# First dense layer of batches 1 to 3 by another chained seven-product scheme, in a fused windowed attention and dense kernel

## The chip, the cores and the metric

The kernel runs on one core of one Trainium2 chip. The metric is the device time of a run in microseconds; with one core that core is also the slowest. Several runs are taken and the median counts.

## The reference

Four batches of eight heads, 768 positions, 64 features a head. Each position attends to the 128 positions up to itself and to the first four positions (the sinks). The result is laid out as 3072 rows of 512 and goes through two dense layers with a squared relu between them. Inputs and output are float32.

```python
scores = np.matmul(q, k.transpose(0, 1, 3, 2)) / np.sqrt(64)     # B=4, H=8, S=768, D=64
keep = is_sink | in_window                                       # 4 sinks, window of 128
a = softmax(np.where(keep, scores, -1e9))
x = np.matmul(a, v).transpose(0, 2, 1, 3).reshape(3072, 512)
h = x @ w_in                                                     # 512 x 2048
r = np.maximum(h, 0.0)
out = (r * r) @ w_out                                            # 2048 x 512
```

## The kernel before, in words

**Order.** Nothing is scheduled by a planner at build time. The program records every step as a numbered `Op` (a step may issue one instruction or many), and `Plan.run` emits the steps in the sequence of a list written out by hand, `ORDER`. Each entry is a step's number, then at times an engine letter (`d` VectorE, `a` ScalarE, `g` GpSimd) where the step may run on several, and `+0` or `+1` where it takes a PSUM tile and may choose between two pools. So the queue of each engine is the order of the list, and an instruction that waits holds back all that stand behind it on its engine. `DUMMIES` adds matmuls that compute nothing ahead of seven of the first steps.

**Rooms.** A `Slot` takes a room of a pool and gives it back after its last reader. PSUM is two pools, `att` and `den`, of two rooms each; a room has two banks of 512 float32 columns. In SBUF there are small pools: `expm` (8 rooms, for exps and temporaries), `r` (3, for relu results), `qs` (6), `qr` (5), `sg`, `osb`, `u`.

**Waits inside a tile.** By default two instructions that touch the same tile are ordered. `touch` removes that order for two accesses of one tile that use different banks, when one is a matmul and the other is not, or when both are by different engines and both were recorded with `alone=True` and with different `part` names.

**Stages.** For each batch: loads of q, k and v on GpSimd's and SyncE's queues; transposes of q and k (L507 on TensorE for batches 0 and 1; for batches 2 and 3 by transposing transfers on SyncE's queue, L461); scores per pair of sequence tiles and head pair (L613); exps on ScalarE (L634); masks (L218 GpSimd, L643 and L646 VectorE); values (L682); reciprocals and norms (L698, L699) into `xn_sb`; a bridge that transposes `xn_sb` into `xT` (L731 on TensorE, or transposing transfers). `copy` (L192 ScalarE, L194 VectorE) moves tiles out of PSUM and casts loaded ones. A batch has three pairs of sequence tiles, 256 positions each.

**First dense layer.** Batch 0 does it as written: `layer1`, 192 matmuls (L763), relu, square. Batches 1 to 3 do it by a seven-product scheme for a 2 by 2 block product: `layer1_fast` forms sums of input blocks (`xs`), `weight_sums_in` once forms sums of weight blocks (`wi`, six in tiles of their own, L810, and four in the place of `w_in`, L818), and `quad` does seven products for four blocks of the result. `FAST` says which pairs go together; a lone pair is first spread into `xd` by ScalarE. There are 18 quads. In a quad, PSUM holds one room of two banks, and a float32 tile `t` keeps a running difference:

1. product 1 into bank 0, product 2 into bank 1; `t` is the copy of bank 0, then `t` minus bank 1 (L936)
2. product 5 starts bank 0 again; `t` minus bank 0 (L936); products 4 and 3 add to banks 1 and 0
3. one relu over both banks, 1024 wide (L951 ScalarE, L953 VectorE); its square (L917, L919)
4. products 6 and 7 add to the banks; one custom VectorE sum over both banks with `t`, bounded below by zero, 1024 wide (L963); its square

**Second dense layer.** Pairs 0 and 1 of batch 0 as written (`layer2`, L984); the others by a chained seven-product scheme (`layer2_chain`, L1233), the very last pair by another (`layer2_fast`, L1094), with sums of weights (L1025) formed once. Results are copied to `osb` and stored from SyncE's queue (L1276).

Of the kernel before, what the change touches and what calls it, by code (L numbers as in the profile page):

```python
# [15 lines left out]
ALU = mybir.AluOpType  # L16
# [5 lines left out]
944 0 1 2 7 8 9 10 11 12 13 14 15 16 17 18 945+0 3 5 19 20 21 6 79 22 23 24 25 55d 56d 57+0 58 59d 60a 83+0 85 103+1  # L22
105 26 27 28 62d 61d 63+1 64 67d 68d 65a 69+0 70 71d 72d 66a 84+1 73a 74a 75+1 76 78d 91+0 86 77a 93 80 113+1 87+0
92+1 89 94 95+0 97 115 88 90 96 98 114+1 99+0 101 117 100d 104+0 81+1 102d 107 82 4 29 106g 30 31 32 33 34 35 36 37 38
39 40 41 42 43 44 45 46 127 47 48 49 50 116d 118d 108d 156+0 109+1 119+1 121 111 162+0 110 120 122 112 123+1 125 124d
126d 157a 163a 158a 164a 168+1 165+0 51 52 53 54 177+0 169a 170d 208g 166a 167a 178d 171+1 179a 172a 128+1 131+0 174+0
173a 132a 129d 319 323 321 175d 324 176d 322 130a 320 159+1 133a 160a 161a 278+0 279 136+1 144+0 145+0 280 281 148 138
146 289+1 149d 139d 274 147d 275 282 290 283 291 292 284 276 277 134+1 137+0 135 286a 140 141d 285 287d 293 150+0 151
294 142+1 196+0 192+1 295 143 193 200+1 198a 202a 195d 197 199d 201 203d 297d 194d 296 298a 152+1 154 204+0 205
212+0+1 153a 155d 189+0 215 206a 213 190a 214 207d 186+0 216 191d 248+0 187d 249d 251+1 209 253a 188d 252a 180+1 181d  # L30
250d 182d 183+0 326 184a 185d 300 301 230+0+1 233 299 288 219+0+1 231 220 304+0 210+0 306a 211 222 305 237+0+0 240
232d 325 302 221 303 223 241d 238 239d 311 307 217+1 254+0 224+0 308a 255 309 218 242+0 225 243 452g 422 423 424 425
426 427 428 429 430 431 432 433 434 234g 235+1 226+0 228 310a 227a 229a 314 236 244+0 246 316a 247a 327 313 245d 329
256+0+1 257 315 328 332 317 330 347+1 333+1 348 334 259 335a 337 312 336 331 338 349a 263+1+1 266 264 339 351 340 341a
350 352 435 436 437 258g 438 439 267g 265g 361+0 353 362 354 363d 260g 364 343 365 366 445 440 453 444 441 355a 356a
342a 448 446 449 442 447 443 451 450 318 344 345 357 375+0 358 376 261+0 359 377a 346a 367 368 379 378 262 380 268+0
270+0 381 382 360a 369a 271a 269 370d 371 272 273d 372 383a 389 373 463+0+0 385 386 466 464 390 408+0 409 394+1 395
410a 391 393 387 411 396a 397 412 456+1+0 413 392 414 398 400 415 374d 388a 457 384a 399 504 458 506 465 467 505 508+0
416a 401 418 419 510a 511 402a 654 655 684g 656 657 658 659 660 661 662 663 664 665 672 459 420 460 685 512a 417a 421a
403a 404 468+0 509 405 513 454+1 469 406 507 514a 455 515 461+0 472+1+0 407a 517 523 542 462 518 519 521 544 675 673  # L40
470 473 546+0 475 543 548a 479+0+0 516 520d 549 480 482 550a 524 481d 545 476d 525 483d 547 495+1+0 551 553 496 552a
498 556 674 676 666 667 668 474g 669 670 499g 471 522 679 488+0+0 555 554 526 497d 484+1 557 491 489 671 492g 490g
477+0 500+0 485 478 559 501 561 527+0 528 529d 563 562 493+0 565 558d 494 534 530 535 531d 566+0 567 532 533a 568d 569
564 570 572 571 536 683 682 677 678 486 502 680 711+0+0 487 503 573 574d 537 538 539d 540 681 541 560 714 712 704+0+0
580+0 581 576 577 582d 583 594 584 585 575a 705 707 688+0+0 713g 715g 706g 708g 689 691 578 586 587 626+1 627 588a
628a 612+0 686+0 613 687 630 596 692 690 595 629 631 716+0 717 589a 614a 632 633 579a 634a 635a 615 590 616 597 617
693+0 694 591 618 636 619 637 592 598+1 599 620a 600a 638 593a 601 622 640+0 641 602 623 642a 736 643 603 644 604 646
605 645 709+0 647 624 740+0 639a 621a 606a 648a 742a 649a 607a 608 609 738 737 650 651 743 739 710 610 611d 741
695+0+0 744a 625a 696 698 652 653d 755 697 699 756 757 745 747 746a 749 748 720+0+0 723 759+0 750 700+0 701 761a 762
751 721 752a 763a 760 722g 753 724g 727+0+1 774 775 758 728 730 725+0 766 764 778+1 779 765a 729d 767 776 726 777 768  # L50
731g 732+1 733 718 719 702 703 754 734 735 793 794 785 770 769 798+1 812+0 799 813 780a 771a 800a 814a 781 782a 797
796 786 772 795 815 801 802 816 817 818 803 783 819 784d 787 820a 804 805 789 822 823 829 826 827 828 791 806a 807a
821a 808 809 788 830+0 831 790a 832a 824 825d 810 858+1 811a 834 872+0 844+1 860a 846a 874a 833 835 836 837 873 845
859 876 838a 839a 886 887 888 875 877 861 840 841 848 862 864 792 773 842 863 847 889 849 878 879 890+0 865 843a 880a
850 882 883 851 892a 881a 866d 867d 884 893 894d 868 869 852a 853a 854 855 870 856 895 891 897 896a 885a 900 857d 871d
# [1345 lines left out]
```

## Time and profile before

| What | Value |
|---|---|
| median of 3 runs | 210.87 us (210.46 to 211.46) |
| span of the profiled execution | 208.3 us; no other time of that execution is given |
| instructions | 5924 |
| TensorE matmul / weight load busy | 200.5 us (96%) / 174.3 us (84%) |
| VectorE / ScalarE / GpSimd busy | 173.1 us (83%) / 135.9 us (65%) / 96.4 us (46%) |
| granted TensorE clock | 1.00 throughout |
| moved by transfers | 26.10 MB |

The span runs from the first to the last recorded instruction of one execution; the median is of runs timed as a whole and is 2.6 us longer. PE is TensorE's matmul side and PEld its weight loads, which overlap; DVE is VectorE, ACT ScalarE, POOL GpSimd, SP SyncE. In a timeline row the first number is the start, the second the time from the start to the end of the group, then engine, line, operation, what is written and read, shapes and count; a bracket names the idle time before it and what ended it. In a row by windows the columns are the stretch, its length, and the busy time of PE, PEld, DVE, ACT and POOL with their instruction counts, then the granted clock and the share and rate of the transfers.

### The profile page before, as it was taken

The page shows a single profiled execution, that of the slowest core. Times are in us where ns is not written, and L with a number is a line of the kernel's source. Part 1 is how long each engine was busy: PE and PEld are TensorE (multiplying, and loading weights), DVE is VectorE, ACT ScalarE, POOL GpSimd, SP SyncE. Part 2 cuts the span into 40 slices and gives each one's busy share as a digit, 9 for nine tenths or more (in the row PEclk, how much of TensorE's full clock was granted, in tenths as well). Part 3 has the DMA queues.
Part 4 walks back from the last instruction along what each step waited for, and adds up shares of the span by engine and source line. Part 5 has one row for each costly group of instructions (what it writes and reads, how often), then busy time and mean ns, then how long its engine had stood idle before and what let it go on. Part 6 is the DMA issues. An engine that isn't in the chain of part 4 may idle for free.

```text
span 208.3 us, 5924 instructions
## 1 busy us (share of the span) xinstructions
PE 200.5 (96%) x2476; PEld 174.3 (84%) x2476; DVE 173.1 (83%) x318; ACT 135.9 (65%) x189; POOL 96.4 (46%) x138
## 2 busy tenths in 40 slices
PE   7989999999998999999999998999999999999993
PEld 7658997457986889989878987999888999998893
DVE  6759268867599998999999987999989598999933
ACT  2695888433749589999987047988856248693110
POOL 7999274599599976689356209000043000000000
PEclk9999999999999999999999999999999999999999
DMA  6999999999999999999999945300204203200115
GB/s 190 260 184 207 173 196 215 166 146 142 261 68 148 131 172 137 181 162 121 154 116 220 109 96 134 148 3 0 50 14 145 50 5 113 88 3 0 50 54 201
DMA packets 93994, 26.10 MB, mean 125 GB/s; under 512 B 86800, under 2 KB 91408, under 8 KB 93968
## 3 DMA queue, kind: packets, MB, share of 16 engines
q0 software_dynamic: 69248, 12.59, 80.2%
q1 hardware_dynamic: 24536, 13.01, 27.9%
q8 instruction: 19, 0.31, 0.6%
q10 hardware_dynamic: 184, 0.14, 0.2%
q14 instruction: 7, 0.06, 0.1%
HBM read 27.30 MB, written 6.29 MB: 161 GB/s over the span
## 4 chain that ended last, share of the span: by engine, by line
PE 82%; DVE 5%; DMA 4%; SPq 3%; ACT 2%; issue 2%; DVEq 0%; ACTq 0%
PE py L1233 26%; PE pm L894 23%; PE pm L763 10%; PE py L984 7%; PE po L682 6%; PE ps L613 4%; DMA qr<-in_q_dram 3%; PE pt L507 2%; PE py L1094 2%; SPq L351 2%; DVE t L936 1%; PE px L731 1%; DMA xT<-xn_sb 1%; SPq L461 1%; ACT expm L634 1%
## 5 line engine op out<-in xcount | busy, mean ns | idle before, releaser
L634 ACT ACTIVATE expm<-ps 128x1024 bf16<-128x1024 f32 (+1 forms) x48 | 43.7, 953 | 7.7 <-PE ps L613 7.5
L218 POOL TENSOR_SCALAR_AFFINE_SELECT expm<-expm 128x512 bf16<-128x512 bf16 x34 | 22.7, 705 | 44.2 <-ACT expm L634 40.4
L894 PEld LDWEIGHTS <-w_in_sb 128*128 128x128 bf16 x384 | 32.2, 114 | 2.0 <-issue 1.9
L1233 PEld LDWEIGHTS <-gT_sb 128*128 128x128 bf16 x288 | 27.2, 98 | 4.7 <-issue 1.4
L917 ACT ACTIVATE gT_sb<-r 128x1024 bf16<-128x1024 bf16 x28 | 28.8, 1054 | 2.5 <-DVE r L963 2.3
L894 PE MATMUL pm<-xs,wi 128*128 128x256 bf16 (+1 forms) x288 | 29.2, 246 | 0.1
L192 ACT ACTIVATE osb<-py 128x256 f32<-128x256 f32 (+1 forms) x30 | 11.9, 399 | 25.0 <-PE py L1233 19.8
L936 DVE TENSOR_TENSOR t<-t,pm 128x512 f32<-128x512 f32 x36 | 23.8, 683 | 3.7 <-PE pm L894 2.9
L894 PEld LDWEIGHTS <-wi 128*128 128x128 bf16 x288 | 24.6, 114 | 1.0 <-DVE xs L852 0.4
L1233 PEld LDWEIGHTS <-sg 128*128 128x128 bf16 x216 | 20.3, 98 | 2.7 <-issue 0.5
L963 DVE CUSTOM_DVE_ANT_1 r<-pm,t 128x1024 bf16<-128x1024 f32 x18 | 21.8, 1218 | 0.5 <-PE pm L894 0.5
L763 PE MATMUL pm<-xT,w_in_sb 128*128 128x256 bf16 x192 | 22.0, 273 | 0.0
L763 PEld LDWEIGHTS <-w_in_sb 128*128 128x128 bf16 x192 | 20.6, 114 | 0.3 <-issue 0.2
L894 PE MATMUL pm<-xs,w_in_sb 128*128 128x256 bf16 (+1 forms) x192 | 19.9, 246 | 1.0 <-DVE t L936 1.0
L951 ACT ACTIVATE r<-pm 128x1024 bf16<-128x1024 f32 x16 | 16.3, 1022 | 4.9 <-DVE osb L194 2.3
L1233 PE MATMUL py<-w_out_sb,gT_sb 128*128 128x256 bf16 x144 | 18.7, 273 | 0.6 <-ACT expm L634 0.6
L1233 PE MATMUL py<-wt,sg 128*128 128x256 bf16 x144 | 18.7, 273 | 0.0
L1233 PE MATMUL py<-wt,gT_sb 128*128 128x256 bf16 x144 | 18.5, 273 | 0.0
L682 PEld LDWEIGHTS <-expm 128*128 128x128 bf16 x352 | 16.6, 97 | 1.9 <-issue 0.6
L682 PE MATMUL po<-v,expm 128*128 128x65 bf16 x352 | 17.8, 193 | 0.3 <-ACT expm L634 0.3
L699 DVE TENSOR_TENSOR xn_sb<-po,rc 128x512 bf16<-128x512 f32 (+1 forms) x28 | 17.2, 615 | 1.0
L984 PE MATMUL py<-w_out_sb,gT_sb 128*128 128x512 bf16 x64 | 14.8, 379 | 0.0
(104 smaller groups left out, 376.9 us busy)
## 6 DMA issues: line engine op xcount, KB each, us to landing
out_dram<-osb SPq DMA_DIRECT2D x11, 512.0 KB, 3.7
v<-in_v_dram POOLq DMA_DIRECT2D x24, 128.0 KB, 6.2
qn<-in_k_dram POOLq DMA_DIRECT2D x20, 128.0 KB, 6.1
qn<-in_q_dram POOLq DMA_DIRECT2D x20, 128.0 KB, 6.5
w_in_sb<-in_moe_w_in_dram POOLq DMA_DIRECT2D x4, 512.0 KB, 9.4
w_out_sb<-in_moe_w_out_dram POOLq DMA_DIRECT2D x4, 512.0 KB, 10.8
qr<-in_k_dram SPq DMA_DIRECT2D x4, 256.0 KB, 5.1
qr<-in_q_dram SPq DMA_DIRECT2D x4, 256.0 KB, 4.8
```

The source lines that it names most:

```text
L218: nc.gpsimd.affine_select(out=e_tile, in_=e_tile, compare_op=ALU.is_ge, fill=fill, base=i - 1, pattern=[[0, n], [1 if i else -1, 128]], ch ...
L634: nc.scalar.activation(out=x[:, :, o:512], in_=bank_t["s", b, s, m][:, :, o:512], func=AF.Exp, scale=scale)
L682: touch(("po", b, s, m0), e, nc.tensor.matmul(pv[:, i, h2, :], lhsT=lhsT, rhs=rhs, start=(n_ == 0), stop=(n_ == len(mms) - 1)), j)
L699: touch(("po", b, s, m0), e, nc.vector.tensor_tensor(out=xn_sb[:, 2 * s:2 * s + 2, 128 * (m0 + j0):128 * (m0 + j0 + nj)].rearrange("p i (j ...
L763: nc.tensor.matmul(pm[:, i, :], lhsT=w_in_sb[:, fb // 4, kb, fb % 4:512:4], rhs=xT[:, c0 // 256:(c0 + cw) // 256, kb, :], start=(kb == 0), ...
L894: touch(tag, e, nc.tensor.matmul(y[:, bk, i, :], lhsT=weights(name, f0 + i, a), rhs=rhs[:, a, :], start=fresh and i == 0 and a == 0, stop= ...
L917: nc.scalar.activation(out=d, in_=x, func=AF.Square)
L936: touch(tag, e, nc.vector.tensor_tensor(out=T["t"], in0=T["t"], in1=T["y"][:, bk], op=ALU.subtract), bk)
L951: touch(tag, e, nc.scalar.activation(out=r, in_=T["y"], func=AF.Relu), 0, 1)
L963: touch(tag, e, nc.vector._custom_dve(TENSOR_ADD_SAT, out=r.rearrange("p b n c -> p b (n c)"), in0=T["y"].rearrange("p b n c -> p b (n c)" ...
L984: touch((b, u), e, nc.tensor.matmul(pm[:, i, :], lhsT=gT_sb[:, fb, 128 * t:128 * t + 128], rhs=w_out_sb[:, fb, :], start=(fb == 0), stop=( ...
L1233: touch((b, u), e, nc.tensor.matmul(region(name), lhsT=x[:, i, :], rhs=w_[:, i, :], start=first and i == 0, stop=i == HB - 1, skip_group_c ...
```

## The change

The first layer of batches 1 to 3 keeps 18 quads and seven products each, with another set of block sums. All sums are chained differences: four `xs` tiles of two blocks for each call (before: three of two blocks and one of four), and four `wi` sums in two halves each, eight instructions (before: ten). A quad keeps three copies of bank 0 at different stages instead of a running difference:

1. products 1 and 2 into banks 0 and 1; copy `c1` of bank 0; the bounded sum of bank 1 and `c1` is the first half of `r1`
2. product 6 adds to bank 0 (after `c1` is taken), product 7 starts bank 1 again (after the first sum); copy `c2`; product 5 adds to bank 0; copy `c3`; the bounded sum of bank 1 and `c3` is the second half of `r1`; square
3. products 3 and 4 add to the banks; a relu of bank 0 and the bounded sum of bank 1 and `c2` fill `r2`; square

So a quad has three copies, three custom sums and one relu, all 512 wide, in place of one copy and two differences 512 wide and a relu and a custom sum 1024 wide. Copies, sums and the relu are recorded with `alone=True` and a `part` name each, so that two of them on different engines are ordered only where they use the same bank (or read each other's result). Each copy may be on ScalarE or VectorE, by the letter in `ORDER`; the custom sums are VectorE's.

`ORDER` is new as a whole: 980 entries for 946, since a quad has more steps, in another sequence for every stage of all four batches, with other engine letters and pool choices. The numbers of matmuls are the same. One cast of batch 0's q goes to GpSimd. Only the first lines of the list are shown here.

```diff
 ORDER = """
-944 0 1 2 7 8 9 10 11 12 13 14 15 16 17 18 945+0 3 5 19 20 21 6 79 22 23 24 25 55d 56d 57+0 58 59d 60a 83+0 85 103+1
-105 26 27 28 62d 61d 63+1 64 67d 68d 65a 69+0 70 71d 72d 66a 84+1 73a 74a 75+1 76 78d 91+0 86 77a 93 80 113+1 87+0
+0 8 7 9 978 1 10 6 56d 979+1 11 3 55d 61d 12 57+0 58 13 14 15 19 20 63+0 62d 59a 21 79 60 22 64 103+1 5 65a 66a 104+0
+16 105 23 67d 68d 83+0 4 69+1 70 107 73d 71 75+1 72a 24 77 113+1 85 74 115 76 91+0 78 80 92+0 84+1 114+1 25 93 94 26
...
-    945: 29, 58: 8, 63: 10, 64: 4, 83: 3, 91: 3, 97: 3,
+    979: 29, 58: 8, 63: 10, 64: 4, 83: 3, 91: 3, 97: 3,
...
-        spec = ((1, A[0][0], A[1][1], ALU.add, (0, 0), (0, 1)), (6, A[1][0], A[0][0], ALU.subtract, (0, 2), (1, 0)),
-                (7, A[0][1], A[1][1], ALU.subtract, (1, 1), (1, 2)))
+        spec = ((1, A[1][0], A[1][1], ALU.add, (0, 0), (0, 1)), (2, 1, A[0][0], ALU.subtract, (0, 2), (1, 0)),
+                (4, A[0][1], 2, ALU.subtract, (1, 1), (1, 2)))
...
-        for name, x, y, old in ((2, A[1][0], A[1][1], 6), (5, A[0][1], A[0][0], 7)):
-            for a in range(2):
+        for a in range(2):
+            def run(e, x=A[1][0], y=A[0][0], a=a):
+                wi_sb[3, a] = x[:, :, a]
+                nc.vector.tensor_tensor(out=x[:, :, a], in0=y[:, :, a], in1=x[:, :, a], op=ALU.subtract)
+            ops["wi", 3, a] = op(key + 0.03 + 0.004 * a, {"dve": 0.7}, run, after=[ops["wi", 1, a]] + last)
...
-        total((1,), lambda: part(0, 0), lambda: part(1, 1), ALU.add, 0)
-        total((4,), lambda: part(1, 0), lambda: part(0, 0), ALU.subtract, 1)
-        total((3,), lambda: part(0, 1), lambda: part(1, 1), ALU.subtract, 2)
-        total((6, 7), lambda: halves[0], lambda: halves[1], ALU.add, 3)
+        o1 = total(1, lambda: part(0, 1), lambda: part(0, 0), 0, [])
+        o2 = total(2, lambda: part(1, 1), lambda: xs[1], 1, [o1])
+        total(3, lambda: part(1, 1), lambda: part(0, 1), 2, [])
+        total(4, lambda: part(1, 0), lambda: xs[2], 3, [o2])
...
-        bs, ts, r1s, r2s = Slot(("den", "att"), 1), Slot("expm", 3), Slot("r", 1), Slot("r", 1)
+        bs, r1s, r2s = Slot(("den", "att"), 2), Slot("r", 1), Slot("r", 1)
...
+        def kept(name, n, after):
+            slot = cs[name] = Slot("expm", 1)
+
+            def run(e):
+                T[name] = bank(slot, "t", [128, nb, hw], FP32)
+                touch(tag, e, copy(e, T[name], T["y"][:, 0]), 0, alone=True, part=name)
+            P.group = ("t", b, ss[0])
+            return op(key(n), {"act": 0.6, "dve": 0.69}, run, after=after, takes=[slot])
...
+        def bounded(r, slot, half, name, n, after, takes, reads=()):
+            def run(e):
+                d = rooms_of(r, slot)[:, half]
+                touch(tag, e, nc.vector._custom_dve(
+                    TENSOR_ADD_SAT, out=d.rearrange("p n c -> p (n c)"),
+                    in0=T["y"][:, 1].rearrange("p n c -> p (n c)"),
+                    in1=T[name].rearrange("p n c -> p (n c)"), s0=3.4028235e38, s1=0.0), 1, alone=True, part=name)
+            P.group = ("t", b, ss[0])
+            return op(key(n), {"dve": 0.69}, run, after=after, takes=takes, reads=[cs[name]] + list(reads))
...
         m1 = product(1, 0, 0, True, [])
         m2 = product(2, 1, 1, True, [])
-        k1 = op(key(1), {"act": 0.6, "dve": 0.64}, first, after=[m1], takes=[ts])
-        k2 = op(key(2), {"dve": 0.7}, less(1), after=[m2, k1], reads=[ts])
-        m5 = product(5, 0, 2, True, [k1])
-        k3 = op(key(3), {"dve": 0.7}, less(0), after=[m5, k2], reads=[ts])
-        m4 = product(4, 1, 3, False, [k2])
-        m3 = product(3, 0, 4, False, [k3])
-        k4 = op(key(5), {"act": 1.04, "dve": 1.25}, relu, after=[m3, m4], takes=[r1s])
-        square(6, "r1", f0, 1, r1s, [k4])
-        m6 = product(6, 0, 6, False, [k4])
-        m7 = product(7, 1, 7, False, [k4])
-        k5 = op(key(8), {"dve": 1.25}, final, after=[m6, m7, k3], takes=[r2s], reads=[bs, ts])
-        square(9, "r2", f0 + 8, 1, r2s, [k5])
+        k1 = kept("c1", 1, [m1])
+        e1 = bounded("r1", r1s, 0, "c1", 2, [m2, k1], [r1s])
+        m6 = product(6, 0, 2, False, [k1])
+        m7 = product(7, 1, 3, True, [e1])
+        k2 = kept("c2", 3, [m6])
+        m5 = product(5, 0, 4, False, [k2])
+        k3 = kept("c3", 5, [m5])
+        e4 = bounded("r1", r1s, 1, "c3", 6, [m7, k3], [])
+        square(7, "r1", f0, 0, r1s, [e1, e4])
+        m3 = product(3, 0, 6, False, [k3])
+        m4 = product(4, 1, 7, False, [e4])
...
+        k4 = op(key(7), {"act": 0.6, "dve": 0.69}, relu, after=[m3], takes=[r2s], reads=[bs])
+        e3 = bounded("r2", r2s, 1, "c2", 8, [m4, k2], [], [bs])
+        e3.after.append(k4)
+        square(9, "r2", f0, 1, r2s, [k4, e3])
```

More of the change, by code (lines that the diff above doesn't have):

```diff
@@ L27 @@
[L27 to L36, printed above, removed]
@@ L897, in run @@
                             skip_group_check=not (fresh and i == 0)), bk)
[L898 to L901 removed]
+            wi = {5: 1, 6: 2, 7: 3, 3: 4}.get(name)
+            need = [ops["wi", wi, a] for a in range(2)] if wi else [w_in_op[i] for i in range(4)]
+            o = op(key(n), {"pe": 0.45}, run, after=after + need + ([sums[x]] if x else landed) + last[-1:],
+                   takes=[bs] if name == 1 else [], reads=[slots[x]] if x else [whole] if len(ss) == 1 else [])
             last.append(o)
```

137 lines of the change are left out of this document (62 added, 75 removed).

## The prediction

> **What bounds the kernel now.** I read the page first (the busy shares), then the busy time by windows, then PE's instructions in order of time at the places where it waits, then the groups by shape.
>
> ```profile
> span 208.3 us, 5924 instructions
> ...
> PE 200.5 (96%) x2476; PEld 174.3 (84%) x2476; DVE 173.1 (83%) x318; ACT 135.9 (65%) x189; POOL 96.4 (46%) x138
> ```
> ```profile
> 0.00:11.40 11.40, 9.45 (x100) 7.80 (x101) 7.32 (x20) 5.78 (x9) 9.74 (x21) 1.00 1.04 222
> ...
> 36.00:63.00 27.00, 26.05 (x264) 18.18 (x263) 19.72 (x32) 13.19 (x21) 21.26 (x30) 1.00 1.90 157
> 63.00:83.00 20.00, 19.97 (x261) 17.58 (x261) 18.97 (x36) 16.53 (x26) 17.20 (x23) 1.00 2.04 146
> 83.00:90.00 7.00, 6.91 (x105) 6.21 (x103) 6.77 (x13) 6.78 (x9) 4.07 (x7) 1.00 1.35 207
> 90.00:119.50 29.50, 29.45 (x440) 25.90 (x441) 28.58 (x57) 22.71 (x32) 18.64 (x24) 1.00 1.90 139
> 119.50:130.00 10.50, 9.53 (x147) 8.30 (x145) 8.12 (x14) 6.61 (x8) 4.94 (x8) 1.00 0.51 112
> ```
>
> The columns are length, then PE, PEld, DVE, ACT and POOL busy with their instruction counts. PE is full from 11.4 us on, at a granted clock of 1.00. DVE is nearly as full wherever a fast first layer runs: 18.97 of 20.0 us, then 6.77 of 7.0. So two engines bound this kernel, PE everywhere and DVE a hair behind it.
>
> "PE busy" hides small waits, because ends of matmuls are modelled. So I price the stream itself by what long runs take on the chain that ended last:
>
> ```profile
> 22.15 6.99 PE pm L763 x64
> ...
> 33.52 1.73 PE py L984 x8
> ...
> 69.66 1.45 PE po L682 x48
> 71.11 0.45 PE px L731 x8
> 72.88 0.55 PE ps L613 x12
> ```
>
> That is 0.109 us for a 256-column matmul, 0.216 for 512, 0.030 for the 65-column ones, 0.056 for 128, and 0.55 for twelve scores. Over the 2476 matmuls this makes 192 us, an estimate. The changed program has the same 2476 matmuls in the same shapes, so PE's stream is 192 us in both. **Only PE's lost time can differ.** I call "work ahead" the stream that stands before an instruction in its program, and "lost" its start less its work ahead. Lost time now:
>
> ```profile
> 19.79 1.91 PE L763 MATMUL pm<-xT,w_in_sb 128*128 128x256 bf16 x16
> ...
> 60.92 0.78 PE L613 MATMUL ps<-qkT 64*128 64x128 bf16 x16
> 62.10 0.34 PE L613 MATMUL ps<-qkT 64*128 64x256 bf16 x4 [0.40 <-ACT r L775]
> 63.02 1.03 PE L1233 MATMUL py<-w_out_sb,gT_sb 128*128 128x256 bf16 x8 [0.57 <-ACT expm L634]
> ...
> 128.26 0.64 PE L894 MATMUL pm<-xs,w_in_sb 128*128 128x128 bf16 x8
> 129.87 0.61 PE L894 MATMUL pm<-xs,w_in_sb 128*128 128x128 bf16 x8 [0.97 <-DVE t L936]
> ```
>
> The second first-layer product starts at 19.79 with 12.9 us ahead of it: 6.9 us are lost in the start. The twenty scores from 60.92 take 0.9 us back to back, yet the next product starts at 63.02: 1.2 us lost. At 128.26 eight matmuls take 0.45 us and the next start at 129.87: 1.2 us lost. About 0.5 us goes between 83 and 90. The rest is steps of 0.1 to 0.3 us, most of them at a change of matmul kind, which both programs have.
>
> **The change, part by part.**
>
> *The arithmetic of a quad.* Each of the 18 quads still has seven products. Rows:
>
> ```profile
> L936 DVE TENSOR_TENSOR t<-t,pm 128x512 f32<-128x512 f32 x36 | 23.8, 683 | 3.7 <-PE pm L894 2.9
> L963 DVE CUSTOM_DVE_ANT_1 r<-pm,t 128x1024 bf16<-128x1024 f32 x18 | 21.8, 1218 | 0.5 <-PE pm L894 0.5
> ...
> L852 DVE TENSOR_TENSOR xs<-xT 128x1024 bf16<-128x1024 bf16 x3 | 2.0, 683 | 0.0
> ```
> ```profile
> L951 ACT ACTIVATE r<-pm 128x1024 bf16<-128x1024 f32 x16 | 16.3, 1022 | 4.9 <-DVE osb L194 2.3 <-PE pm L894 1.9 <-DVE r L953 0.4
> ...
> L192 ACT ACTIVATE t<-pm 128x512 f32<-128x512 f32 x15 | 8.5, 597 | 0.2
> ```
> ```profile
> 29.96 1.89 DVE L810 TENSOR_TENSOR wi<-w_in_sb 128x1024 bf16<-128x1024 bf16 x3
> ```
>
> Out go 36 subtractions (0.683) and 18 wide sums (1.218): 46.5 us of DVE. In come 54 sums at half width. The trace has no custom sum 512 wide; the plain one of that width is 0.683 and half of 1.218 is 0.61. I take 0.683, since 1.218 at twice the width leaves the same fixed part: 36.9 us. By the new order DVE also does 10 more copies out of PSUM (0.68, 6.8 us) and 8 more squares by the list of instructions (11 with batch 0, at 0.68, 7.5 us), and saves two of the ten weight sums and about 1.8 us of input sums (the 1024-wide one becomes a 512-wide one). With what moves elsewhere DVE is within +3 us of 173 busy; ACT changes 17 wide relus (1.02) for 15 half ones and 26 copies (0.60) and gives 11 squares away: within 5 us of before. No engine is relieved. Instructions on DVE overlap: three of 0.683 take 1.89, so they start 0.60 apart, 0.085 closer than their duration.
>
> A rule speaks against these half-width passes. In rows: two plain passes of 512 cost 1.366, one of 1024 costs 1.218, so a split costs 0.15, or 0.07 by starts. The Trainium skill (Perfetto Trace Analysis, Optimizing Scalar/DVE Operations) gives about 125 ns of access overhead to a DVE instruction on PSUM and advises larger operations when the engine is saturated, as DVE is here. By that figure the roughly eleven extra PSUM passes of DVE would cost about 1.4 us, an estimate from that page; the trace's two prices bracket its 125 ns.
>
> *The start.* The new order makes PE do all attention values of the second tile pair ahead of the first first-layer product, and DVE converts q before k:
>
> ```profile
> 3.56 0.47 DVE L194 CAST qs<-qr 128x512 bf16<-128x512 f32 x1
> ...
> 4.71 0.43 DVE L194 CAST qs<-qr 128x512 bf16<-128x512 f32 x1 [0.68 <-DMA qr<-in_q_dram]
> ...
> 7.02 2.20 DVE L194 CAST qs<-qr 128x512 bf16<-128x512 f32 x4 [1.28 <-DMA qr<-in_q_dram]
> 7.37 1.72 ACT L634 ACTIVATE expm<-ps 128x768 bf16<-128x768 f32 x2 [0.48 <-PE ps L613]
> ```
> ```profile
> L634 ACT ACTIVATE expm<-ps 128x1024 bf16<-128x1024 f32 x32 | 31.3, 1023 | 6.1 <-PE ps L613 5.9
> ...
> L634 ACT ACTIVATE expm<-ps 128x768 bf16<-128x768 f32 x16 | 12.7, 812 | 1.6 <-PE ps L613 1.5
> ...
> L192 ACT ACTIVATE qkT<-pt 128x512 bf16<-128x512 bf16 x12 | 6.7, 595 | 7.7 <-PE pt L507 7.7
> ```
>
> The q cast stood behind q's landing at 4.71; now k's, ready at 3.56, queues behind it on DVE, and the first copy out of the transposes queues behind the second pair's q, which lands at 7.02. So the first exp moves from 7.37 to about 8.8: cast to 7.6, copy to 8.3, scores. From there ACT does eight exps (four of 1.02, four of 0.81), one copy (0.6) and about 0.8 of small work: 17.5 us. Then 1.7 us of values and transposes: the first first-layer product starts near 19.2 with 11.1 us ahead, 8.1 lost. One conversion goes to POOL, where none is shown; its copies lie at
>
> ```profile
> L259 POOL COPY mask<-tri 128x256 bf16<-128x256 bf16 x1 | 1.4, 1427 | 0.0
> ...
> L254 POOL COPY sg<-sg 128x512 bf16<-128x512 bf16 x1 | 0.6, 611 | 0.1
> ```
>
> 0.6 to 1.4 us; I take 0.7, the same width. It delays the small ACT work by up to 0.7 us at the upper end and nothing at the lower. A second bound does not depend on this walk. The transposes of tiles 4 and 5 of batch 0 stand at 20.3 us of work ahead in the new order. They read q tiles whose load is
>
> ```profile
> L372 POOL DMA_DIRECT2D qn<-in_q_dram x1: 893/893/893, 17.8 to 17.8; - x1
> ...
> DMA to landing us min/median/max: 10.2/10.2/10.2
> ```
>
> landed at 28.0. The loads stand in the same order on POOL's queue, so at least 28.0 - 20.3 = 7.7 us are lost there, 0.3 less if POOL's earlier first issues shift the queue. Against 6.9 the start costs **+1.0 us** (+0.6 to +1.6).
>
> *Waits that go.* The 1.2 us at 61 to 63 came from batch 0's last relu, queued on ACT before the exps. In the new order its squares are done with 51.9 us ahead, and the product that needs them has 54.3: gone, **-1.2**. The 1.2 us at 128 belong to a chain over two subtractions in a lone quad of batch 2; the new chain has other work between its products: **-1.2**, next late is nothing by my walk there (22.4 us of DVE in 27 of PE). The 0.5 us of 83 to 90 is replaced by the next item: **-0.5**.
>
> *Batch 1's quads.* Here a copy gates each next product of its bank, and behind a waiting copy or sum on DVE are queued the norms, whose transposes PE waits for. From the first DVE copy (66.0 us of PE work ahead) to the sum that the third second-layer product needs (86.2), DVE has 36 instructions. At the mean of the present stage (18.97/36 = 0.527) they take 19.0 of 20.2 us. But DVE comes late: 29 instructions before them, at the 28.58/57 = 0.50 of the calmer stage, take 14.6 from 52.3, so it starts at 66.9. Then there is no slack, and each dependent pair stalls. Walking copy, sum and product hop by hop, PE waits for the last square of the first pair 0.6 us, for a mask 0.25, and five more times 0.15 to 0.3: **+2.0**. Ends: 0 if starts stay 0.60 apart (19.0 + 0.9 < 20.2), and 4 if every instruction costs its duration (36 x 0.085 = 3 more, with the 0.9).
>
> *The rest.* SP's stores stand at other places between the transposing loads; the store of batch 0's third pair now has eight key and query transposes behind it, but these are wanted some 12 us later. Batches 2 and 3: I find waits of 0.1 to 0.4 us, **+0.5** together (0 to 1.5). The tail after PE's last product has the same instructions.
>
> Sum: 1.0 - 1.2 - 1.2 - 0.5 + 2.0 + 0.5 = +0.6 us on a span of 208.3. The runs' median, 210.87, is 2.6 above the span that the page gives, and I add the change to the median: **211.4 us**, +0.3%. A measurement of this kernel can tell about 0.5% (1.05 us).
>
> **The rivals.**
>
> *DVE takes over as the bound in batch 1.* Mechanism: late copies and sums push the norms, and those the transposes, so DVE's in-order queue sets the pace at its durations. Price: the upper ends, 4 us there and 1.3 in the rest, instead of 2.5: 214.2 us. It decides from the point where DVE is over 1 us late at the first copy. For it: 18.97 of 20.0 us busy already. Against: starts 0.60 apart. Chance 0.30. The advice of the Trainium skill on larger operations, cited above, would come out as this case.
>
> *Copies and sums keep ahead of PE.* Batch 1 costs nothing, the two waits go, the start costs 0.8: 208.3 - 2.1 on the span, 208.8 us. For it: the finer steps free a bank after 0.6 instead of 1.02 or 1.22 us. Against: DVE's late start. Chance 0.27.
>
> *The freed ordering does nothing*, since the copies and sums of one quad depend on each other anyway; then only the order counts and the result lies in the forecast's range. Chance 0.03, counted as no change.
>
> **How the numbers follow.** Forecast, 0.40, its own range 209.6 to 212.8. Range over the cases: 208.6 to 214.4, with a tenth outside at each end. Faster by over 0.5% (under 209.8): the second rival and 0.02 of the forecast, 0.29. Within: 0.25 of the forecast and the third rival, 0.28. Slower (over 211.9): the first rival and 0.13 of the forecast, its upper third, 0.43.
>
> **What would show it.** After: the transposes of tiles 4 and 5 not before 28.0 us; no wait over 0.4 us where batch 0's last pair begins its second layer; in batch 1 PE waiting for DVE's sums, squares and xn_sb by about 2 us in all; DVE busy within 3 us of 173. I am wrong if PE waits under 0.5 us in batch 1's quads, if it waits over 3.5, or if a transfer I called hidden ends a wait of PE.

## The result, and the profile after

The changed kernel takes 211.80 us (median of 9 runs, 211.10 to 212.51) against 210.82 us (9 runs of before): a ratio of 1.0057, 95% interval [1.0035, 1.0080]. The forecast was 211.4 us, +0.3%, range 208.6 to 214.4. The total came out close to it; the terms did not. The profiled execution of after has a span of 210.1 us against 208.3. That is 1.8 us where the medians differ by 1.0: the execution of before that was profiled is one of its faster ones. In runs with both numbers the time is 1.7 us above the span, not the 2.6 that I had read off the median.

The page of after, busy shares as in the first fence of the prediction:

```profile
span 210.1 us, 5968 instructions
...
PE 202.0 (96%) x2476; PEld 175.5 (84%) x2476; DVE 174.5 (83%) x337; ACT 133.2 (63%) x204; POOL 96.4 (46%) x137
```

DVE is 1.4 us busier and ACT 2.7 less, inside the bounds that the prediction gave (3 and 5). The groups by shape say what a quad now costs on each engine:

```profile
L941 DVE CUSTOM_DVE_ANT_0 r<-pm,t 128x512 bf16<-128x512 f32 x54 | 36.0, 685 | 3.5 <-PE pm L891 1.9 <-ACT t L192 1.2 <-issue 0.2
L194 DVE COPY t<-pm 128x512 f32<-128x512 f32 x13 | 8.9, 687 | 2.0 <-PE pm L891 1.4 <-POOL expm L218 0.5
...
L192 ACT ACTIVATE t<-pm 128x512 f32<-128x512 f32 x41 | 23.9, 599 | 13.1 <-PE pm L891 12.0 <-PE po L682 0.6
L966 ACT ACTIVATE r<-pm 128x512 bf16<-128x512 f32 x15 | 8.8, 596 | 1.9 <-PE pm L891 1.7
```

The half-width bounded sum takes 0.685 us; I had taken 0.683 from the plain subtraction of that width. Now the timeline of after at the places that the prediction had looked at (PE, and one row of ACT):

```profile
1.59 3.28 PE L1368 MATMUL pw<-tri 128*128 128x128 bf16 x29 [1.59 <-DVE tri L224]
6.05 0.61 PE L507 MATMUL pt<-ident,qs 128*128 128x128 bf16 x4 [1.19 <-DVE qs L194]
...
9.65 0.62 PE L507 MATMUL pt<-ident,qs 128*128 128x128 bf16 x4
10.81 1.93 ACT L634 ACTIVATE expm<-ps 128x1024 bf16<-128x1024 f32 x2
...
12.16 0.84 PE L507 MATMUL pt<-ident,qs 128*128 128x128 bf16 x12
20.52 1.67 PE L763 MATMUL pm<-xT,w_in_sb 128*128 128x256 bf16 x13
...
29.80 0.61 PE L507 MATMUL pt<-ident,qn 128*128 128x128 bf16 x8
...
63.31 0.62 PE L613 MATMUL ps<-qkT 64*128 64x128 bf16 x12
63.86 0.29 PE L572 MATMUL pk<-qkT,kblk 128*32 128x256 bf16 x4
64.08 1.04 PE L989 MATMUL py<-w_out_sb,gT_sb 128*128 128x512 bf16 x4
...
132.39 0.40 PE L572 MATMUL pk<-qkT,kblk 128*32 128x512 bf16 x4 [0.16 <-ACT expm L634]
133.07 0.61 PE L891 MATMUL pm<-xs,wi 128*128 128x128 bf16 x8 [0.28 <-ACT t L192]
```

The first first-layer product starts at 20.52 with 11.1 us ahead of it, so 9.4 us are lost in the start (before: 6.9, forecast: 8.1). Between 60 and 66 no row has a bracket: the wait of before is gone. At 132 there is a new one. Lost time, as the prediction defined it, at some positions of PE's program (work ahead in us, against the program with 29 first dummies; worked out from all of PE's starts), for the two kernels and for the experiments that follow. Differences in the text are taken before rounding:

| work ahead | 13 | 50 | 60 | 90 | 110 | 125 | end |
|---|---|---|---|---|---|---|---|
| before | 6.9 | 7.2 | 8.9 | 9.9 | 10.4 | 12.1 | 12.8 |
| after | 9.4 | 10.1 | 10.8 | 11.9 | 12.4 | 13.6 | 14.6 |
| fewer dummies in before | 7.8 | 8.1 | 9.8 | 10.8 | 11.3 | 11.9 | 12.6 |
| after, freed ordering taken back | 9.4 | 9.9 | 10.8 | 14.0 | 14.7 | 17.2 | 21.9 |
| after, bias and dummies | 7.9 | 8.4 | 9.3 | 10.4 | 11.0 | 12.1 | 13.3 |
| after, bias only | 9.5 | 10.0 | 10.9 | 12.0 | 12.5 | 13.7 | 14.6 |
| after, mended start | 8.0 | 8.5 | 9.4 | 10.5 | 11.0 | 13.8 | 14.7 |
| after, copies on DVE | 11.4 | 11.9 | 12.8 | 16.0 | 16.5 | 18.5 | 19.5 |

The change loses 2.6 us in the start and wins 0.8 us back behind it.

### The profile page after: what moved, and what is told of

The parts are those of the page before. It is cut to its first block, busy times and chain, and to the rows that moved or that the text cites. A ratio compares the mean times of both kernels' runs of the same rounds, so it can differ in the third digit from the quotient of the medians.

```text
span 210.1 us, 5968 instructions
## 1 busy us (share of the span) xinstructions
PE 202.0 (96%) x2476; PEld 175.5 (84%) x2476; DVE 174.5 (83%) x337; ACT 133.2 (63%) x204; POOL 96.4 (46%) x137
## 4 chain that ended last, share of the span: by engine, by line
PE 84%; ACT 6%; DVE 5%; DMA 2%; issue 2%; SPq 0%; ACTq 0%
PE py L1238 27%; PE pm L891 22%; PE pm L763 10%; PE po L682 6%; PE py L989 6%; PE ps L613 5%; ACT expm L634 3%; PE pt L507 3%; DVE r L941 2%; DMA qr<-in_q_dram 2%; PE py L1099 2%; ACT t L192 1%; PE px L731 1%; PE pt L185 1%; PE pk L572 1%
## 5 line engine op out<-in xcount | busy, mean ns | idle before, releaser
L634 ACT ACTIVATE expm<-ps 128x1024 bf16<-128x1024 f32 (+1 forms) x48 | 43.4, 951 | 11.7 <-PE ps L613 11.2
L218 POOL TENSOR_SCALAR_AFFINE_SELECT expm<-expm 128x512 bf16<-128x512 bf16 x32 | 21.9, 715 | 44.7 <-DVE gT_sb L916 18.5
L941 DVE CUSTOM_DVE_ANT_0 r<-pm,t 128x512 bf16<-128x512 f32 x54 | 36.0, 685 | 3.5 <-PE pm L891 1.9
L192 ACT ACTIVATE t<-pm 128x512 f32<-128x512 f32 x41 | 23.9, 599 | 13.1 <-PE pm L891 12.0
L914 ACT ACTIVATE gT_sb<-r 128x1024 bf16<-128x1024 bf16 x20 | 21.1, 1059 | 1.4 <-DVE r L941 1.1
L891 PE MATMUL pm<-xs,wi 128*128 128x256 bf16 (+1 forms) x192 | 21.1, 246 | 0.3 <-ACT t L192 0.3
L891 PE MATMUL pm<-xs,w_in_sb 128*128 128x256 bf16 (+1 forms) x192 | 21.1, 246 | 0.0
L192 ACT ACTIVATE osb<-py 128x256 f32<-128x256 f32 (+1 forms) x28 | 10.9, 402 | 15.4 <-PE py L1238 13.9
L1238 PE MATMUL py<-wt,gT_sb 128*128 128x256 bf16 x144 | 18.5, 273 | 0.0
L699 DVE TENSOR_TENSOR xn_sb<-po,rc 128x512 bf16<-128x512 f32 (+1 forms) x28 | 17.2, 615 | 1.0
L989 PE MATMUL py<-w_out_sb,gT_sb 128*128 128x512 bf16 x64 | 15.3, 380 | 0.0
L613 PE MATMUL ps<-qkT 64*128 64x128 bf16 (+1 forms) x256 | 14.4, 238 | 0.9 <-ACT qkT L192 0.8
```

Source lines behind the costliest of these rows:

```text
L192: return nc.scalar.activation(out=dst, in_=src, func=AF.Copy)
L218: nc.gpsimd.affine_select(out=e_tile, in_=e_tile, compare_op=ALU.is_ge, fill=fill, base=i - 1, pattern=[[0, n], [1 if i else -1, 128]], ch ...
L613: nc.tensor.matmul(ps[:, h2, o:o + w], lhsT=qkT_sb[r, m, 1, c, :], rhs=qkT_sb[r, m, 0, qb:qb + w // 128, :], start=(i == 0 and not biased) ...
L634: nc.scalar.activation(out=x[:, :, o:512], in_=bank_t["s", b, s, m][:, :, o:512], func=AF.Exp, scale=scale)
L699: touch(("po", b, s, m0), e, nc.vector.tensor_tensor(out=xn_sb[:, 2 * s:2 * s + 2, 128 * (m0 + j0):128 * (m0 + j0 + nj)].rearrange("p i (j ...
L891: touch(tag, e, nc.tensor.matmul(y[:, bk, i, :], lhsT=weights(name, f0 + i, a), rhs=rhs[:, a, :], start=fresh and i == 0 and a == 0, stop= ...
```

## The experiments

Each was timed in five rounds beside the kernel before; a ratio is to before, so 1.0057 is the changed kernel's.

### More dummies, fewer dummies

```diff
-    979: 29, 58: 8, 63: 10, 64: 4,        # after
+    979: 41, 58: 8, 63: 10, 64: 4,        # more dummies in after
-    945: 29, 58: 8, 63: 10, 64: 4,        # before
+    945: 8, 58: 8, 63: 10, 64: 4,         # fewer dummies in before
```

> The changed kernel with 41 instead of 29 dummy matmuls at the very start, which fills the pause of PE from 4.66 to 6.05 us and adds no other work. In its trace the 128-column matmuls start 0.107 us apart until 9.98 us and 0.056 apart from 11.29 us on; before's switch between 6.36 and 6.99 us. Theory 1, the pause restarts PE's slow phase: the switch then comes near 6.7 us, the first exp at about 9.4 instead of 10.81, and the first layer begins with about 8.3 us lost instead of 9.4. The transposes of tiles 4 and 5 wait for a q load that landed at 28.96 us with 20.3 us ahead, so no more than 0.8 us of this can last: 0.6 to 0.8 us less in all, near 211.1. Rival 1, the slow phase has nothing to do with the pause: the switch stays near 10 us and the time at 211.8. Rival 2, the start is faster but DVE then comes late in batch 1's quads as I had forecast, and gives it back there: start as in theory 1, end at 211.8.

> The kernel before with 8 instead of 29 dummy matmuls at the start, so that PE pauses from about 2.2 us to 4.34 us; nothing else is changed. Theory 1, a pause restarts the slow phase: 128-column matmuls start 0.107 apart until 8.2 to 9.4 us instead of 6.4, first exp about 1.0 us later than 7.37, first layer 0.8 to 1.3 us later, total 0.7 to 1.3 us over before. Rival, the slow phase ends at a set time after the start or after a count of matmuls not reached by pausing: the switch stays between 6.4 and 7.0 and the total is that of before within 0.3.

With 41 dummies after took 212.81 us, ratio 1.0125 [1.0085, 1.0165], 1.0 over after. With 8 dummies before took 210.20, ratio 0.9988 [0.9962, 1.0013]: no difference. Neither total is theory 1's, and yet both traces show its mechanism. With 41 dummies the 128-column matmuls go from 0.107 to 0.056 us apart at 4.55 us instead of behind 10. But PE then runs ahead, waits from 9.20 to 10.76 for the score bias, which GpSimd builds until 10.7 in this order, and the busy time by windows shows what follows (the clock is the column behind POOL):

```profile
4.55:9.20 4.65, 4.22 (x67) 3.50 (x66) 3.15 (x6) 2.29 (x4) 4.40 (x8) 1.00 1.15 254
9.20:10.76 1.56, 0.22 (x3) 0.10 (x2) 0.70 (x2) 1.44 (x2) 1.44 (x5) 1.00 1.63 244
10.76:15.00 4.24, 3.98 (x33) 2.62 (x32) 2.37 (x5) 2.46 (x5) 4.22 (x8) 0.60 1.68 188
```

The granted clock of the third window is 0.60: PE is back at half step (matmuls 0.107 us apart), and the start loss is 9.5 us, nothing won. All six runs of it have a mean granted clock of 0.989 to 0.992, so this is not one execution's accident (of after's nine runs, two have such a clock). Its profile also loses 1.0 us more than after's behind 110 us of work ahead, at a wait for a transposing load that is told below. In before with 8 dummies PE pauses until 4.10:

```profile
4.10 0.61 PE L507 MATMUL pt<-ident,qs 128*128 128x128 bf16 x4 [1.80 <-DVE qs L194]
4.51 1.06 PE L185 MATMUL pt<-ident 128*128 128x128 bf16 x8
...
9.28 0.63 PE L185 MATMUL pt<-ident 128*128 128x128 bf16 x4
```

Four matmuls take 0.63 us still at 9.28 (0.39 at full step), the switch comes at 10.1, and the start loss grows by 0.9 us as theory 1 had it. That the total does not move is in the table: by 125 us of work ahead the loss is gone, since the wait at 129.87 (1.1 us, for the subtraction of a lone quad) shrank to nothing. VectorE in before, then with 8 dummies, shows what that wait was:

```profile
128.27 0.95 DVE L852 TENSOR_TENSOR xs<-xT 128x512 bf16<-128x512 bf16 x1 [0.64 <-DMA xT<-xn_sb]
129.14 0.68 DVE L936 TENSOR_TENSOR t<-t,pm 128x512 f32<-128x512 f32 x1
```
```profile
128.47 0.46 DVE L852 TENSOR_TENSOR xs<-xT 128x512 bf16<-128x512 bf16 x1
128.86 0.67 DVE L936 TENSOR_TENSOR t<-t,pm 128x512 f32<-128x512 f32 x1
```

In before the subtraction stands in VectorE's queue behind an input sum, and that sum waits for a transposing transfer. With 8 dummies the transfer was there in time, and the subtraction ran 0.28 us earlier than in before although PE was 0.9 us later. A loss ahead of a wait that does not move with it costs nothing.

### The start of before in the new order, long and short

```diff
-0 8 7 9 978 1 10 6 56d 979+1 11 3 55d 61d 12 57+0 58 ...       # after
+978 0 1 2 7 8 9 10 ... 55d 56d 57+0 58 59d 60a 83+0 ...         # before's entries,
+...  179a 172a 128+1 131+0  (long)    ... 102d 107 82  (short)  # up to here; then the rest of the new order
```

> The changed kernel with the start of the order of before (all entries up to the transposes of tiles 4 and 5 of batch 0, with the engines and pools chosen there), then the rest of the new order. Theory 1, the start is where the change loses and the rest of the new order keeps what it gains: lost time 6.9 us at the first layer, 7.7 at most behind the loads, the total 1.6 to 2.3 us less than changed: 209.5 to 210.2, under before. Rival, DVE sets the pace in batch 1's quads and the late start only hid it: PE waits appear there for 1.5 to 2 us together and the total stays within 0.5 of 211.8.

> The changed kernel whose first entries, up to the scores of the second pair and its sink exp, stand in the order and with the engines of the kernel before; from there the new order follows (the earlier run took the old start some twelve matmul steps further, into the first layer, and lost 2.9 us at relus between 34 and 38 us). Theory, the start can be had without breaking the rest: first exp near 7.2 us as in the kernel before, start loss 7.2 to 7.8 us instead of 9.4, nothing over 0.4 us lost between 24 and 45 us, end 1.6 to 2.2 us under the changed kernel: 209.6 to 210.2. Rival, the exps of the second pair on ScalarE end no earlier (8 exps and 17 us of work from the first one) and the start loss is 8.0 as with the mended start: 210.6 to 211.1. Second rival, the mixed order stalls at the relus as in the longer one: 212.5 or more.

The long one took 214.02 us, 1.0149 [1.0102, 1.0196]; the short one 212.39, 1.0057 [1.0031, 1.0083]. Both miss. The long one stalls where the two orders meet:

```profile
34.97 1.91 PE L763 MATMUL pm<-xT,w_in_sb 128*128 128x256 bf16 x16 [1.17 <-ACT r L775]
38.20 0.62 PE L613 MATMUL ps<-qkT 64*128 64x128 bf16 x12 [1.32 <-DVE r L777]
```

The short one does not stall there, but in its start PE pauses three times for 1.2 to 1.3 us and falls to half step just ahead of the first layer, which begins at 21.00:

```profile
15.00:19.00 4.00, 2.67 (x42) 1.79 (x42) 2.89 (x9) 3.38 (x5) 3.33 (x7) 0.90 1.31 205
19.00:21.00 2.00, 2.00 (x41) 2.00 (x38) 0.95 (x3) 0.00 (x0) 2.00 (x4) 0.50 1.24 205
```

So neither run says what the start is worth to the rest; the next three do.

### Bias early, with and without dummies, and five moves

```diff
-... 11 3 55d 61d 12 57+0 ... 103+1 5 65a 66a         # after: 5 builds the bias on GpSimd
+... 11 3 5 55d 61d 12 57+0 ... 103+1 65a 66a         # bias only; with 979: 41 bias and dummies
-0 8 7 9 978 1 10 6 56d 979+1 11 3 55d ... 83+0 4 69+1
+978 0 8 7 9 1 10 6 55d 56d 979+1 11 3 5 ... 83+0 74 4 69+1   # mended start, 29 dummies
```

> The changed kernel with GpSimd's building of the score bias directly behind the identity (there the queue stands still until 3.04 us) instead of behind the value sums and loads (8.73 to 10.84 us), and with 41 first dummies. Theory 1: in the run with 41 dummies alone PE was at full step from 4.55 us but paused 1.56 us at 9.2 us for the bias and fell back to half step; with the bias early there is no such pause, the first layer starts 0.7 to 1.4 us earlier than 20.5, the loads come at most 0.5 us later, and the end is 0.4 to 1.0 us under the changed kernel: 210.8 to 211.4. Rival: the casts and copies of q and k set the pace whatever PE's step is: first layer within 0.3 us of 20.5, end at 211.8.

> The changed kernel with the bias built early on GpSimd and the 29 dummies unchanged, to part the two edits of the last run. Theory, the step of PE: the pause from 4.7 to 6.0 us stays, PE's 128-column matmuls start 0.107 us apart until about 10 us, first layer at 20.0 to 20.5 us, total 211.3 to 211.9. Rival, the loads: the value loads start 0.7 us later on GpSimd's queue behind the bias, so the last k lands at 9.4 us instead of 10.8 and GpSimd's cast runs a microsecond earlier, and this alone gives the whole gain: first layer at 19.0, total 210.6 to 210.9.

> The changed kernel with its start mended by five moves and nothing else: the bias built early on GpSimd, the first memsets for PE's dummies ahead of the others, k cast before q on VectorE as in the kernel before, GpSimd's cast of q put two places earlier, and the 29 dummies kept. Theory, the start is what the change loses and the rest of the new order is 0.8 us better than before's: PE has no pause at 4.7 us, first exp near 8.0 us, start loss 7.0 to 7.5 us, end 1.9 to 2.4 us under the changed kernel: 209.4 to 209.9, under the kernel before. Rival, the landing of the last q and k and the exps on ScalarE set the start (17.5 us from the first exp), or a later wait (loads, batch 1's quads) takes it back: 210.5 to 211, as with bias and dummies.

Bias and dummies: 210.67 us, 1.0018 [0.9997, 1.0039]. Bias only: 211.31, 1.0040 [1.0013, 1.0067]. Mended start: 211.05, 1.0003 [0.9975, 1.0031]. PE in the first and the second of these:

```profile
1.59 4.46 PE L1368 MATMUL pw<-tri 128*128 128x128 bf16 x41 [1.59 <-DVE tri L224]
6.16 0.40 PE L507 MATMUL pt<-ident,qs 128*128 128x128 bf16 x4
...
19.00 3.75 PE L763 MATMUL pm<-xT,w_in_sb 128*128 128x256 bf16 x32
```
```profile
6.31 0.61 PE L507 MATMUL pt<-ident,qs 128*128 128x128 bf16 x4 [1.45 <-DVE qs L194]
...
20.58 2.65 PE L763 MATMUL pm<-xT,w_in_sb 128*128 128x256 bf16 x22
```

Without the pause four transposes take 0.40 us at 6.16 and the first layer starts at 19.00; with it they take 0.61 and it starts at 20.58, as in after. The last k landed early in both, at 9.4 and 9.2 us (10.8 in after), so the rival, the loads, is out: what counts in the start is the pause. In the runs the gap of the two is 0.64 us and their intervals overlap; the 1.6 us is a reading of the two traces. The mended start has no pause either and starts the first layer at 19.10, 8.0 us lost. Its first exp comes at 9.07, as with bias and dummies (9.02), and not near 8.0: on PE the first scores stand behind the transposes of the second pair, whose casts on VectorE wait for loads until 6.53 and 7.39. The chain over ScalarE's exps takes the rest, as its rival said. Its profile then loses 1.6 us elsewhere:

```profile
123.05 0.45 PE L613 MATMUL ps<-qkT 64*128 64x128 bf16 x8 [1.37 <-DMA qkT<-qn]
```

Such a wait, 0.6 to 1.6 us, is in six profiles of variants of the new order and absent in after's own and three others. It is for the last of six transposing loads that SyncE issues back to back: it landed at 123.0 us here and at 121.3 in the run with bias and dummies, whose PE was as far. With one profile of each kernel it can't be told whether the kernels or their executions differ here; why it varies was not settled.

No variant of the new order beats before: the best two equal it within their intervals.

### The freed ordering taken back

```diff
-                touch(tag, e, copy(e, T[name], T["y"][:, 0]), 0, alone=True, part=name)
+                touch(tag, e, copy(e, T[name], T["y"][:, 0]), 0)
```

(the same for the bounded sum and the relu)

> The changed kernel with copies, bounded sums and relu of a quad ordered by the whole tile again (recorded without alone and part), order and scheme unchanged: the freed ordering taken back alone. Theory, the freed ordering does nothing since copies and sums of one quad depend on each other anyway: within 0.3 us of 211.8. Rival, it matters where ScalarE's copy of bank 0 and VectorE's sum of bank 1 run side by side: the second sum of r2 then waits for the relu and the third copy for the first sum, 18 quads with up to 0.1 us each on PE: 1 to 2 us slower, 212.8 to 213.8.

It took 219.22 us, 1.0426 [1.0390, 1.0461]: 7.4 us slower than after, far beyond both theories. The group of the bounded sums:

```profile
L941 DVE CUSTOM_DVE_ANT_0 r<-pm,t 128x512 bf16<-128x512 f32 x54 | 36.2, 687 | 11.4 <-ACT r L966 5.1 <-PE pm L891 3.3 <-ACT t L192 2.1
```

The idle time ahead of the sums is 11.4 us instead of 3.5, of which 5.1 is for the relu of the other bank, which is not among the releasers named in after. I had priced one quad's wait at 0.1 us because the steps of one quad depend on each other. But a sum that waits for a relu holds all of VectorE's queue, the sums and norms of other quads with it; by the table PE loses 2.1 us more than in after between 60 and 90, 1.3 more between 110 and 125 (0.9 of it the wait for the transposing load) and 3.7 more behind 125.

### Scheme and order exchanged

```diff
-m1 m2 c1 e1 m6 m7 c2 m5 c3 e4 square m3 m4 relu e3 square      # new scheme, names of the diff
+m1 m2 k1 k2 m5 m4 k3 m3    k4 square m6 m7      k5 square      # old scheme in those places
-m1 m2 k1 k2 m5 k3 m4 m3 k4    square m6 m7 k5      square      # old scheme
+m1 m2 c1 e1 m6 c2 m7 m5 c3 e4 square m3 m4 relu e3 square      # new scheme in those places
```

> The seven products, weight sums and input sums of the kernel before, put into the order of the changed kernel: each old step stands where the new step that does its part stands (the first difference at the first bounded sum, the second at copy c2, the wide relu at the second sum, the wide sum at the last one); twelve steps had to move ahead of a step that reads them. Start and second layers are those of the changed kernel. Theory 1, the scheme itself is worth little and the start carries the loss: 211.0 to 212.5, start loss 9.4 us as in the changed kernel. Theory 2, the new order needs the short steps: the wide relu (1.02) and the wide sum (1.22) hold both banks of a room, PE waits for them in each of the 18 quads: 213 to 217. Rival, the scheme costs what I had priced in batch 1: 209.5 to 210.5.

> The new scheme put into the order of the kernel before: copy c1 where the old copy stood, the first bounded sum at the first difference, c2 (on ScalarE) at the second, c3 and the second sum at the wide relu, the relu and the last sum at the wide sum; 37 entries stand a few places later since temporaries take more rooms of expm. The start is that of before. Theory 1, the start carries the loss of the change and the scheme is neutral: start loss 6.9 us, total 209.5 to 211.5. Theory 2, an order made for the other scheme costs more than the start: PE waits in the quads, 212 to 216, with the start still at 6.9 us.

The old scheme in the new order took 232.48 us, 1.1041 [1.1016, 1.1066]; the new scheme in the old order 239.95, 1.1399 [1.1365, 1.1433]. Theory 2 in both, at many times its price. The waits of PE by what released them, first the former, then the latter:

```profile
PE pm L893 <- ACT r L950: 4.3, 4, 1.3
PE pm L893 <- DVE t L935: 3.9, 8, 1.1
```
```profile
PE pm L893 <- DVE r L943: 8.8, 8, 2.4
PE pm L893 <- ACT t L194: 6.0, 5, 1.9
```

PE's first-layer products wait for just the steps that took another's place: the wide relu and the subtractions in one, the sums and copies in the other. Neither exchange is a fair price of a scheme alone; what they show is that an order made for one scheme cost the other 20 to 30 us, in the one placing of its steps that was tried.

### More work on VectorE, and one exp ahead

```diff
-350 353 339d ... 363+0 355 356 ... 381 361 ... 455 385 372 ... 387      # after
+350 353d 339d ... 363+0 355d 356 ... 381d 361 ... 455 385d 372 ... 387d # copies of batch 1 on DVE
-595 646 737 590 703 647 711 597                                         # after
+595 711 590 646 737 703 647 597                                         # 711: the exp at 131.53 us
```

> The changed kernel with five copies of batch 1's first quads moved from ScalarE to VectorE (5 starts of 0.60 = 3.0 us more on VectorE between 81 and 95 us, as much less on ScalarE). In the trace VectorE is busy 20.05 of 21.0 us there with 0.8 us idle in front of copies and sums. Theory 1, VectorE stands just short of the bound there: 2.0 to 3.0 us more PE waits, of which up to 0.9 us may be absorbed at the wait at 132 us: 213.0 to 214.8. Rival, the quads wait for PE's products and not for VectorE, the slack is larger than the busy share says: under 0.7 us, 211.8 to 212.5.

> The changed kernel with one exp of batch 3 (712 of the chain at 131.5 us on ScalarE) put ahead of the copy that waits there for a product until 131.0 us; the engines' other orders are the same. In the trace PE loses 0.33 us at 132.4 (sink scores of batch 3, PSUM room held by that exp) and 0.59 at 133.1 (a copy queued behind it). Theory 1: both go, the product after it runs 0.7 to 0.9 us earlier and this stays to the end: 210.9 to 211.2. Rival: the next thing is as late (values of batch 3 wait for GpSimd's masks, a transposing load lands at 135): 211.6 to 211.8.

Five copies more on VectorE: 214.55 us, 1.0191 [1.0148, 1.0234], 2.8 us over after for 3.0 us of added work. Windows of after and of this kernel, then PE of this kernel:

```profile
77.00:98.00 21.00, 20.90 (x286) 19.39 (x284) 20.05 (x38) 18.25 (x28) 12.84 (x21) 1.00 1.75 152
```
```profile
79.00:100.00 21.00, 19.13 (x242) 17.23 (x241) 20.61 (x39) 13.68 (x20) 13.20 (x21) 1.00 1.43 156
```
```profile
89.14 0.22 PE L682 MATMUL po<-v,expm 128*128 128x65 bf16 x2 [0.61 <-DVE rc L698]
...
92.85 0.60 PE L891 MATMUL pm<-xs,wi 128*128 128x256 bf16 x4 [0.25 <-DVE t L194]
95.25 0.60 PE L891 MATMUL pm<-xT,wi 128*128 128x256 bf16 x4 [0.80 <-DVE t L194]
```

After has PE and DVE both full (20.90 and 20.05 of 21.0 us); here PE falls to 19.13 and waits for DVE. The profiled execution, the slowest of its six runs, lost 2.0 us more in its start too, with the same start order as after: the q that GpSimd casts landed late, PE waited 1.53 us for the cast until 15.06, and from 16.30 to 19.70 the granted clock was 0.50. So the table is read by differences: between 60 and 90 PE loses 2.1 us more than in after. VectorE stood just short of the bound in batch 1, as theory 1 said.

The exp put ahead (711 in the order, called 712 in the text above): 212.22 us, 1.0088 [1.0062, 1.0114], nothing won. The exp has a wait of its own now and the copy, queued behind it, is later than it was:

```profile
131.95 0.81 ACT L634 ACTIVATE expm<-ps 128x768 bf16<-128x768 f32 x1 [0.67 <-DVE r L941]
...
134.71 0.49 PE L891 MATMUL pm<-xs,wi 128*128 128x128 bf16 x6 [1.15 <-ACT t L192]
```

It needs a room of `expm`, and the room that comes free is that of a copy which a VectorE sum has yet to read. I had looked at the engine's queue and not at the rooms.

## Why the prediction was right, and where not

**The arithmetic of a quad** held: 0.685 for the half-width sum, so two of them cost 0.15 more than one of full width, as the two rows of the prediction had it; PE and VectorE, the two bounds, were not relieved. Two slips stood in the working: ScalarE gave up 16 wide relus, not 17, by the row that the prediction shows, and the sum comes to 211.5 us, not 211.4. Neither changes the account.

**The start** was the term mis-sized: +1.0 forecast, +2.6 measured. The step that failed is "so the first exp moves from 7.37 to about 8.8": it came at 10.81. I gave PE's transposes and dummies the step that they have in a running PE. In fact PE paused from 4.66 to 6.05 us for the q cast and made its next 37 matmuls 0.107 us apart, until 10 us. Without that pause (bias and dummies) the start costs 1.0 us over before, which is what I had for the moved casts and values alone; the other 1.5 is the half step. The second bound, tiles 4 and 5 not before 28.0 us, was not reached: they start at 29.80.

**Waits that go.** At 61 to 63 the forecast -1.2 measured -1.0 (from 50 to 60 us of work ahead, 1.7 lost before and 0.7 after). At 128 the forecast -1.2 measured -0.5. The mechanism was wrong in part: I read the wait as a chain over two subtractions, but by the rows above the second one stood behind an input sum that waited 0.64 us for a transposing transfer and then took 0.95 us, against 0.46 with 8 dummies. That is the 1.1 us, and little of it belongs to the old scheme. The wait went, but "next late is nothing by my walk" was wrong too. An exp and a copy on ScalarE cost 0.9 us at 132, of which up to 0.3 may be the ordinary change of matmul kind.

**Batch 1's quads**, forecast +2.0, and -0.5 for what they replace, measured +0.1 from 60 to 90, wrong by the test that the prediction itself set (under 0.5). The walk assumed no slack at all. The lower end that I had written beside it, starts 0.60 apart with 19.0 + 0.9 under 20.2, is what happened: copies, sums and relus in after start 0.60 apart (77.29, 77.89, and 83.94, 84.54, 85.14). The five moved copies show that the slack is as thin as I thought and yet was enough.

**The rest**, +0.5 forecast: 0.3 from 13 to 50 and 0.2 behind 125.

So +0.6 forecast; 2.6 - 1.0 - 0.5 + 0.1 + 0.5 = +1.7 of the 1.8 between the two traces, and +1.0 between the medians. The total came close by luck, because errors had opposite signs: the start too cheap by 1.6 and the wait at 128 by 0.7, batch 1 too dear by 1.4.

**The rivals.** DVE as the bound did not come in after; the copies on DVE show that 3 us more would have brought it. Copies and sums that keep ahead of PE were right about batch 1 and wrong about the total, because of the start. That the freed ordering does nothing was wrong by 7.4 us in this order, though it could not have been seen in the profile of before, which has no such order.

## What to carry to other kernels

Price the first microseconds by the steps that the instructions take there, not by those of the full stream, and count a pause of PE in the start as work at half step behind it (1.5 us here). Ordering inside one tile is not paid once by its own chain: the waiting instruction stands in front of everything else on its engine. When the row that ends a wait has itself just waited, follow it one step further: the subtraction at 129.14 was late because of a transfer. An order written out by hand belongs to one set of steps; a part of it exchanged alone tells of the seam more than of the part.

## What the runs showed of the hardware that I had not expected

In the 14 profiled kernels, 128-column matmuls start 0.107 us apart at first and 0.056 later. In seven without a pause over 0.7 us before the switch (before, 41 dummies, both old starts, bias and dummies, mended start, new scheme in the old order) the step changes 4.0 to 7.0 us after the start of the span. In the six where PE pauses from 4.66 us (after and five variants) it changes at 9.5 to 10.1, and with 8 dummies, a pause from 2.1 to 4.1, at 10.1. The clock record of each trace begins with this change; ahead of it there is no entry, and the views print 1.00, in the table of before too. Read the first step from the starts of matmuls.

Later half steps are in the record, each 3.4 us long at a granted clock of 0.50 (the entry at a trace's very end left out). Four kernels have one in their start (41 dummies, both old starts, copies on DVE), after pauses of 0.9 to 1.8 us between starts of matmuls. The new scheme in the old order has three in its middle, after pauses of 2.4 to 2.8 us, and none after pauses of 1.6 and 1.2 us at 7.0 and 11.2.

The Trainium skill (TensorE: Matmul & The Clock Gate, Part 1: The HAM clock gate) describes a gate that halves the array's clock until a window of about 3.4 us has been busy, with 106.7 and 55.6 ns between such matmuls; the steps agree. Its rule lets the gate fall back after an idle window of that length; in three kernels here pauses of 0.9 to 1.6 us, less than half of it, sufficed, so the measurement decides. That a pause restarts the phase is shown by the pairs with and without dummies; what in a later pause brings the half step back, its length, its place or the kind of matmuls around it, is not.
